# Second tables on ScalarE, another order at the end of a convolution's head, and one slot more between two transposes

## The chip, the cores and the metric

The kernel runs on one core of a Trainium2 chip. The metric is the device time of one execution in microseconds; lower is better. Five engines work side by side, each on its own list of instructions: TensorE (PE; its weight loads are shown as PEld), VectorE (DVE), ScalarE (ACT), GpSimd (POOL), and SyncE (SP), which here only issues DMA transfers. ACT issues some transfers too (ACTq).

## What is computed

```
u = x * v                                        # x, v: (2, 12480, 128) float32
h = (relu(pos_emb @ w1) @ w2) * exp(-0.01*pos)   # one filter for both batches
y = irfft(rfft(u, 2S) * rfft(h, 2S))[:, :S]      # S = 12480, along the sequence
z = (x * y).reshape(24960, 128)
g = z @ w_in                                     # w_in: (128, 2048)
out = max(0.01*g, g) @ w_out                     # w_out: (2048, 128)
```

## The kernel before

The long convolution is a Fourier transform in two steps (a matrix over one part of the index, a turn by phases, a matrix over the other part), and the rest is a two-layer network over 24960 tokens. In time:

- **Stage A** (0 to about 180 us) runs over 16 chunks `c`. It loads x, v and positions of batch 0, multiplies (`uh`), transforms (`a`, L370), adds and subtracts on VectorE (`o`, L106 and L108) and stores to DRAM. At c = 2 it loads the tables `mb` and `mi` of the second step. From c = 6 to 10 the generator `turned` (L160) is stepped once a chunk: it loads phases (`ph`, L164), forms products and sums of cosines and sines (`pr`, `cs`, L170 to L175), scales blocks of the identity by them (`rm`, L181), and from these builds a second set of tables with TensorE.
- **Stage B** (about 185 to 350 us) runs over 25 chunks of frequencies: the hidden layer of the filter (`ep` L714, `es` L717, `hp` L756), the forward matrix (`up` L123), the product with the filter (`ta`, `pin`, L131 and L132), then for the chunk before it the backward matrix (`dp`, L151, in `back_halves`). `dp` has two PSUM tiles, s = 0 and 1. Each is the sum of two matmuls, ri = 0 and 1, and each matmul has 64 rows: s = 0 uses rows 0 to 63 of `pin` and of the table, s = 1 rows 64 to 127. `back_evac` (L203) copies both to `ct`, and `store_back` (L199) stores `ct` in DRAM on ACT's queue. The preparation of the network's weights and pieces of batch 1's convolution (the generator `conv`; its matmuls are L408, its copies L104, its stores `scr1b` L421) are mixed in.
- **The end of the head** (347 to 366 us): the last chunk's `dp` and `ct`, the rows of `ct` that the first tile needs, straight into `cin` (`last_c`, L593), and the loads of the next tiles from what was stored (L565, L569, L586). Then tile 0: `join_hi` (L607) and `join_lo` (L616, L618) form `cp`, on VectorE for tile 0 and on GpSimd for all others; `front(0)` transforms (`yp`, L828), multiplies by x (`zt`, L831), transposes (`zp`, L836), and copies (`zf` L839 and L841, `zh` L847, `zl` L848), and the first matmul of the network, `mh` (L855), can start.
- **The main loop** runs over 50 blocks of 512 tokens times 16 slots, 800 slots. A slot `m1` has three matmuls (`mh`, L855 to L857), then relu and splitting on ACT and DVE; a slot `m2` three more (`acc`, L887 to L889), a few slots behind. The convolution's tiles t = 1 to 63 are fitted in between: `front(t)` in two halves, `yp` and `zt` three slots ahead of slot `ends[t]`, `zp` to `zl` at `ends[t]`; the joins 11 slots ahead (8 for the first two tiles of a batch); the loads at slots that follow from `ends` too. The list `ends` is made backwards: a tile is finished four slots before the block that needs it, and at least eight slots before the next tile. Each block's result is finished during the next block, in slots 2 to 6: `ot` at slot 2, transposes `op` (L911) and the copy `os` (L913) at slot 4, stores behind that. `yp`, `zp` and `op` share one PSUM buffer (tag `io`, one buffer), so each waits until the one before it has been read.

The lists are static: an engine takes its instructions in the order in which the program wrote them.

Of the kernel before, what the change touches and what calls it, by code (L numbers as in the profile page):

```python
# [8 lines left out]
F32 = mybir.dt.float32  # L9
# [4 lines left out]
ALU = mybir.AluOpType  # L14
# [16 lines left out]
def tile_conv_mlp(ctx, tc, x, v, pos_emb, w1, w2, w_in, w_out, cf, cr, cg, cb, ci, cw, out):  # L31
# [78 lines left out]
    def run(g):  # L110
        for _ in g:
            pass
# [32 lines left out]
    def back_halves(dp, pin, c):  # L145

        for j, w in halves(c):
            for ri in range(2):
                for s in range(2):
                    rows = slice(HB * s, HB * s + HB)  # L150
                    nc.tensor.matmul(dp[s][:, w], mi2[j][rows, ri, :], pin[rows, ri, w],  # L151
                                     start=(ri == 0), stop=(ri == 1))

# [5 lines left out]

    def turned(pool, psum, m2, m1):  # L160

        ph = pool.tile([128, 2, 2], F32, tag="ph0", name="ph0", bufs=1)
        for h in range(2):
            nc.sync.dma_start(out=ph[HB * h:HB * h + HB],  # L164
                              in_=cf[0, :, 0, :].rearrange("m (r k) -> m r k", r=2)[:, :, 0:KH + 1:KH])
        yield
        pr = pool.tile([128, 2, 2], F32, tag="pr", name="pr", bufs=1)
        cs = pool.tile([128, 3], F32, tag="cs", name="cs", bufs=1)
        tt = nc.vector.tensor_tensor
        tt(out=pr[:, 0, :], in0=ph[:, :, 1], in1=ph[:, :, 0], op=ALU.mult)  # L170
        tt(out=pr[:, 1, 0:1], in0=ph[:, 1, 1:2], in1=ph[:, 0, 0:1], op=ALU.mult)
        tt(out=pr[:, 1, 1:2], in0=ph[:, 0, 1:2], in1=ph[:, 1, 0:1], op=ALU.mult)
        tt(out=cs[:, 0:1], in0=pr[:, 0, 0:1], in1=pr[:, 0, 1:2], op=ALU.add)
        tt(out=cs[:, 1:2], in0=pr[:, 1, 1:2], in1=pr[:, 1, 0:1], op=ALU.subtract)
        tt(out=cs[:, 2:3], in0=pr[:, 1, 0:1], in1=pr[:, 1, 1:2], op=ALU.subtract)  # L175
        yield
        rm = pool.tile([128, 2, HB], F32, tag="rm", name="rm", bufs=1)
        for h, a, b in ((0, 0, 1), (1, 2, 0)):
            r = slice(HB * h, HB * h + HB)
            for i, q in enumerate((a, b)):  # L180
                nc.vector.tensor_scalar_mul(rm[r, i, :], ident[r, r], cs[r, q:q + 1])  # L181
        yield
        tp = psum()
        for i, t in enumerate((m2[:, 0], m2[:, 1], m1[:, 0], m1[:, 1])):
            nc.tensor.transpose(tp[:, i, :], t, ident)
        ts = pool.tile([128, 4, 128], F32, tag="ts", name="ts", bufs=1)
        nc.scalar.copy(ts, tp)
        yield
        rp = psum()
        for i in range(4):  # L190
            nc.tensor.matmul(rp[:, i, :], ts[:, i, :], rm.rearrange("p r m -> p (r m)"), start=True, stop=True)
        nc.scalar.copy(mi2[1], rp[:, 0:2])
        nc.scalar.copy(mi_h[1], rp[:, 2:4])
        nc.vector.tensor_tensor(out=mi_l[1], in0=rp[:, 2:4], in1=mi_h[1], op=ALU.subtract)
        yield
# [3 lines left out]
        eng.dma_start(out=scr2[b][k0:k0 + n].rearrange("k r m e -> (r m) k e"),  # L199
                          in_=ct[:, :n].rearrange("p k s d -> p k (s d)"))  # L200

    def back_evac(dp, ct, n, other=None):

        for s in range(2):
            (s and other or nc.scalar.copy)(ct[:, :n, s, :], dp[s][:, :n * D].rearrange("p (k d) -> p k d", d=D))
            yield


    with tc.manual_schedule():
# [22 lines left out]
        with ExitStack() as st:  # L232
# [81 lines left out]
            for c in range(NC0):  # L314
                if c + 3 < NC0:
                    load_a(c + 3)
                    if (c + 3) * MC % PQ == 0:
                        load_pos((c + 3) * MC // PQ)
                if c == 2:
                    nc.sync.dma_start(out=mb, in_=cb)  # L320
                    nc.sync.dma_start(out=mi, in_=ci)
                    for s in range(2):
                        for ri in range(2):
                            nc.sync.dma_start(out=mi2[0][HB * s:HB * s + HB, ri], in_=ci[HB * ri:HB * ri + HB, s])
                if c == 6:
                    nc.scalar.mul(mi, mi, 1 / 0.99)
                    for m, mh, ml in ((mb.rearrange("p s r q -> p s (r q)"), mb_h, mb_l), (mi, mi_h[0], mi_l[0])):
                        nc.scalar.copy(mh, m)
                        nc.vector.tensor_tensor(out=ml, in0=m, in1=mh, op=ALU.subtract)
                    turn_ = turned(sba, lambda: psa.tile([128, 4, 128], F32, tag="pp", name="tp"), mi2[0], mi)  # L330
                if 6 <= c < 11:
                    next(turn_, None)
                for f in late:
                    f()
# [286 lines left out]
        with ExitStack() as st:  # L621
# [97 lines left out]
            def evac(c):  # L719
                ct = sbb.tile([128, KC, 2, D], F32, tag="ct", name="ct", bufs=2)  # L720
                k0, n = chunk(c)
                end = c == ORD[-1]
                run(back_evac(dps.pop(c), ct, n, nc.vector.tensor_copy if end else None))
                if c in ORD[-2:]:
                    last_c(ct, k0, n, (nc.sync, nc.scalar if end else nc.sync))
                store_back(0, c, ct, nc.scalar)

            eh, dps = {}, {}
            first_c = upper_c(0)
# [54 lines left out]
                    f()  # L784
                late.clear()

            ahead(A1)
            dps[ORD[-1]] = two("d")
            back_halves(dps[ORD[-1]], pins.pop(ORD[-1]), ORD[-1])
            evac(ORD[-1])  # L790
            load_c(1)
            mult_a(2)
            ahead(A2)
            run(wprep)
            ahead(A3)


# [126 lines left out]
        first = [next(pieces_of(t))[0] for t in range(total)]  # L924
        ends, e = {}, NTL * NF
        for t in reversed(range(1, total)):
            e = min(e - 8, first[t] * NF - 4)
            ends[t] = e
        steps = {}

# [33 lines left out]
        SLOTS = ends[NT] - 14  # L964
        done = AHEAD
        frt = front(0)
        join_hi(0)
        join_lo(0)
        next(frt)
        load_tile(2)  # L970
        fetch_a(3)
        for _ in range(4 * A4):
            next(conv)
        run(frt)
        for _ in range(4 * A5):
# [98 lines left out]
```

## Time and profile before

| | us |
|---|---|
| median of three runs | 1732.74 |
| fastest, slowest | 1730.29, 1736.19 |
| profiled execution, its own time | 1735.8 |
| span of its instructions | 1734.0 |
| stage A, stage B, end of head, main loop (about) | 180, 170, 19, 1368 |

Times in the profile count from the start of the span. A row of a timeline has the start, the busy time, the engine, the line in the kernel, the operation with what it writes and reads, and in square brackets how long the engine had been idle and what released it. A row of a list of waits has who waited for whom: the total in us, how often, and the longest. A matmul of 4-byte data (L151, L408, L828) shows as two records, each with its weight load, so its counts in the trace are twice the program's.

### The profile page before, as it was taken

How to read it: one execution, taken by the hardware profiler on the slowest of the kernel's cores; microseconds unless marked ns; L12 is line 12 of the kernel's file. 1: busy time of each engine (PE TensorE's matmuls, PEld its weight loads, DVE VectorE, ACT ScalarE, POOL GpSimd, SP SyncE). 2: the span in 40 equal slices, each digit the busy share in tenths (PEclk: the TensorE clock that was granted, in tenths of full speed). 3: DMA queues.
4: the chain of work that ended last, by engine and by line, in shares of the span. 5: the costliest groups of instructions: out<-in, count | busy, mean ns of one | idle time of the engine just before them, and what ended most of it. 6: DMA issues, size and time to landing. Idle time of an engine off the chain costs nothing.

```text
span 1734.0 us, 27418 instructions
## 1 busy us (share of the span) xinstructions
PE 1650.2 (95%) x9185; PEld 1327.1 (77%) x9185; DVE 1108.7 (64%) x1705; ACT 985.4 (57%) x2005; POOL 833.0 (48%) x858
## 2 busy tenths in 40 slices
PE   6788799889999999999999999999999999999998
PEld 5777455478888887877788777877787878787878
DVE  3586588744554565555555554577777777777775
ACT  1222354434444466666667666566666666666666
POOL 3444122243444277777768675343644454345430
PEclk9889899989999999999999999999999999999999
DMA  8898899964665475556565551222212122111200
GB/s 225 247 263 242 281 322 331 306 201 148 206 182 175 120 200 160 167 154 194 149 175 167 157 150 64 77 67 62 65 43 81 44 70 70 60 53 56 73 18 20
DMA packets 166679, 253.27 MB, mean 146 GB/s; under 512 B 14622, under 2 KB 119346, under 8 KB 163466
## 3 DMA queue, kind: packets, MB, share of 16 engines
q1 hardware_dynamic: 146378, 225.81, 44.8%
q10 hardware_dynamic: 20160, 25.70, 4.3%
q8 instruction: 73, 1.20, 0.3%
q14 instruction: 68, 0.56, 0.1%
HBM read 167.95 MB, written 83.43 MB: 145 GB/s over the span
## 4 chain that ended last, share of the span: by engine, by line
PE 78%; DMA 9%; DVE 5%; issue 3%; SPq 2%; ACT 2%; POOL 1%; ACTq 0%; POOLq 0%; DVEq 0%
PE mh L855 11%; PE mh L857 10%; PE mh L856 10%; PE acc L889 10%; PE acc L887 10%; PE acc L888 10%; PE cv L137 4%; PE yp L828 4%; PE cv L408 3%; DMA ft<-in_cf_dram 2%; DMA xt<-in_x_dram 2%; PE op L911 2%; DMA scr<-o 1%; PE zp L836 1%; DMA scr<-ct 1%
## 5 line engine op out<-in xcount | busy, mean ns | idle before, releaser
L862 DVE SCALAR_TENSOR_TENSOR rl<-mh,rh 128x512 fp32r<-128x512 f32 (+2 forms) x400 | 270.1, 677 | 311.3 <-ACT rh L861 306.9
L872 DVE TENSOR_TENSOR rl<-r,rh 128x512 fp32r<-128x512 f32 (+1 forms) x400 | 329.5, 837 | 113.3 <-ACT rh L871 105.7
L861 ACT ACTIVATE rh<-mh 128x512 fp32r<-128x512 f32 (+2 forms) x400 | 235.2, 590 | 211.7 <-PE mh L857 197.3
L867 ACT ACTIVATE r<-mh 128x512 f32<-128x512 f32 (+1 forms) x400 | 235.7, 590 | 184.8 <-PE mh L857 168.0
L855 PE MATMUL mh<-zh,w_in_h 128*128 128x512 f32 (+3 forms) x800 | 329.8, 412 | 1.9 <-ACT zh L847 1.3
L857 PE MATMUL mh<-zh,w_in_l 128*128 128x512 f32 (+3 forms) x800 | 310.5, 388 | 0.0
L887 PE MATMUL acc<-rh,w_out_h 128*128 128x512 f32 (+3 forms) x800 | 310.3, 388 | 0.0
L856 PE MATMUL mh<-zl,w_in_h 128*128 128x512 f32 (+3 forms) x800 | 310.0, 388 | 0.0
L889 PE MATMUL acc<-rh,w_out_l 128*128 128x512 f32 (+3 forms) x800 | 310.0, 388 | 0.0
L888 PE MATMUL acc<-rl,w_out_h 128*128 128x512 f32 (+3 forms) x800 | 308.3, 385 | 0.0
L848 POOL TENSOR_TENSOR zl<-zf,zh 128x390 fp32r<-128x390 f32 (+24 forms) x110 | 75.7, 702 | 349.7 <-ACT zh L847 349.5
L618 POOL TENSOR_TENSOR cp<-cq,cp 98x256 f32<-98x256 f32 x252 | 212.4, 843 | 19.8
L607 POOL TENSOR_TENSOR cp<-cin 98x256 f32<-98x256 f32 x126 | 104.5, 850 | 162.8 <-PE yp L828 118.7
L855 PEld LDWEIGHTS mh<-zh,w_in_h 128*128 128x128 f32 x800 | 151.1, 189 | 37.0 <-issue 9.9
L857 PEld LDWEIGHTS mh<-zh,w_in_l 128*128 128x128 f32 x800 | 150.8, 189 | 32.1
L888 PEld LDWEIGHTS acc<-rl,w_out_h 128*128 128x128 f32 x800 | 150.4, 188 | 32.1 <-DVE rl L872 0.6
L889 PEld LDWEIGHTS acc<-rh,w_out_l 128*128 128x128 f32 x800 | 150.3, 188 | 31.5
L887 PEld LDWEIGHTS acc<-rh,w_out_h 128*128 128x128 f32 x800 | 150.4, 188 | 30.4
L856 PEld LDWEIGHTS mh<-zl,w_in_h 128*128 128x128 f32 x800 | 151.5, 189 | 24.5 <-POOL zl L848 0.7
L869 DVE CAST rh<-r 128x512 fp32r<-128x512 f32 (+1 forms) x200 | 114.3, 572 | 38.4 <-ACT r L867 35.8
L871 ACT CAST rh<-r 128x512 fp32r<-128x512 f32 (+1 forms) x200 | 122.1, 611 | 6.4
L616 POOL TENSOR_TENSOR cq<-cin 98x256 f32<-98x256 f32 x126 | 113.3, 899 | 1.0 <-DMA cin<-scr 1.0
(154 smaller groups left out, 2359.0 us busy)
## 6 DMA issues: line engine op xcount, KB each, us to landing
cin<-scr SPq DMA_DIRECT2D x318, 98.0 KB
hd<-hspec SPq DMA_DIRECT2D x48, 512.0 KB
scr<-o SPq DMA_DIRECT2D x32, 588.0 KB
bin<-scr SPq DMA_DIRECT2D x23, 768.0 KB
scr1b<-o SPq DMA_DIRECT2D x32, 392.0 KB
hspec<-hs ACTq DMA_DIRECT2D x48, 256.0 KB
scr<-ct ACTq DMA_DIRECT2D x24, 512.0 KB
xm<-in_x_dram SPq DMA_DIRECT2D x128, 96.0 KB
```

The source lines that it names most:

```text
L618: eng.tensor_tensor(out=cp[:, p, w], in0=cq[:, p], in1=cp[:, p, 1], op=op)
L855: nc.tensor.matmul(hp, w_in_h[:, fs], zh, start=True, stop=False)
L856: nc.tensor.matmul(hp, w_in_h[:, fs], zl, start=False, stop=False)
L857: nc.tensor.matmul(hp, w_in_l[:, fs], zh, start=False, stop=True)
L861: nc.scalar.activation(out=rh, in_=hp, func=AF.Relu)
L862: nc.vector.scalar_tensor_tensor(out=rl, in0=hp, scalar=0.0, in1=rh, op0=ALU.max, op1=ALU.subtract)
L867: nc.scalar.activation(out=r, in_=hp, func=AF.Lrelu, alpha=0.01)
L871: nc.scalar.copy(rh, r)
L872: nc.vector.tensor_tensor(out=rl, in0=r, in1=rh, op=ALU.subtract)
L887: nc.tensor.matmul(ap, w_out_h[:, f, :], rh, start=(f == 0 and at0[k] >= S), stop=False)
L888: nc.tensor.matmul(ap, w_out_h[:, f, :], rl, start=False, stop=False)
L889: nc.tensor.matmul(ap, w_out_l[:, f, :], rh, start=False, stop=(f == NF - 1))
```

## The change

Four edits.

1. `back_halves` runs s in the outer loop and ri in the inner one: both matmuls of rows 0 to 63 come first, then both of rows 64 to 127. This holds for all 25 chunks of stage B.
2. `turned`: the products, sums and scaled blocks are made by ScalarE (12 small operations) instead of VectorE; `ph` is loaded as 50 contiguous numbers of each of two parts rather than two numbers picked out of each; its load is issued at c = 2, ahead of `mb` and `mi`, and all later steps come one chunk earlier (c = 6 to 9).
3. End of the head: both copies of the last `ct` are ScalarE's (the second was VectorE's); its store goes on SP's queue, behind the rows of `last_c`, instead of ACT's; seven pieces of `conv` come before the last `dp` and one behind `evac` (eight before), which moves the `scr1b` stores behind those rows; `join_hi(0)` stands ahead of the next pieces, and one more piece stands ahead of `join_lo(0)`.
4. Tiles are seven slots apart instead of eight. In 16 places, where two tiles fall to one block (t = 1, 5, 9, 13, 17, 21, 26, 30, 32, 36, 40, 44, 48, 53, 57, 61), the earlier of the two moves one slot back.

The core of the diff:

```
     def back_halves(dp, pin, c):
         for j, w in halves(c):
-            for ri in range(2):
-                for s in range(2):
-                    rows = slice(HB * s, HB * s + HB)
+            for s in range(2):
+                rows = slice(HB * s, HB * s + HB)
+                for ri in range(2):
                     nc.tensor.matmul(dp[s][:, w], mi2[j][rows, ri, :], pin[rows, ri, w],
                                      start=(ri == 0), stop=(ri == 1))
...
     def turned(pool, psum, m2, m1):
-        ph = pool.tile([128, 2, 2], F32, tag="ph0", name="ph0", bufs=1)
+        ph = pool.tile([128, 2, KH + 1], F32, tag="ph0", name="ph0", bufs=1)
         for h in range(2):
             nc.sync.dma_start(out=ph[HB * h:HB * h + HB],
-                              in_=cf[0, :, 0, :].rearrange("m (r k) -> m r k", r=2)[:, :, 0:KH + 1:KH])
+                              in_=cf[0, :, 0, :].rearrange("m (r k) -> m r k", r=2)[:, :, :KH + 1])
         yield
...
-        tt(out=pr[:, 0, :], in0=ph[:, :, 1], in1=ph[:, :, 0], op=ALU.mult)
-        tt(out=pr[:, 1, 0:1], in0=ph[:, 1, 1:2], in1=ph[:, 0, 0:1], op=ALU.mult)
...
+        for i, (a, b, c, d) in enumerate(((c1, c0, s1_, s0_), (c0, s1_, c1, s0_))):
+            nc.scalar.mul(pr[:, i:i + 1], a, b)
+            if i:
+                nc.scalar.mul(pr[:, 2:3], c, d)
+                nc.scalar.mul(pr[:, 2:3], pr[:, 2:3], -1.0)
+                nc.scalar.add(cs[:, 2:3], pr[:, 1:2], pr[:, 2:3])
+                nc.scalar.mul(cs[:, 1:2], cs[:, 2:3], -1.0)
+            else:
+                nc.scalar.mul(pr[:, 2:3], c, d)
+                nc.scalar.add(cs[:, 0:1], pr[:, 0:1], pr[:, 2:3])
...
-                nc.vector.tensor_scalar_mul(rm[r, i, :], ident[r, r], cs[r, q:q + 1])
+                nc.scalar.mul(rm[r, i, :], ident[r, r], cs[r, q:q + 1])
...
                 if c == 2:
+                    turn_ = turned(sba, lambda: psa.tile([128, 4, 128], F32, tag="pp", name="tp"), mi2[0], mi)
+                    next(turn_)
                     nc.sync.dma_start(out=mb, in_=cb)
...
-                if 6 <= c < 11:
+                if 6 <= c < 11 - 1:
                     next(turn_, None)
...
-                run(back_evac(dps.pop(c), ct, n, nc.vector.tensor_copy if end else None))
+                run(back_evac(dps.pop(c), ct, n))
                 if c in ORD[-2:]:
                     last_c(ct, k0, n, (nc.sync, nc.scalar if end else nc.sync))
-                store_back(0, c, ct, nc.scalar)
+                store_back(0, c, ct, nc.sync if end else nc.scalar)
...
-            ahead(A1)
+            for _ in range(4 * A1 - 1):
+                next(conv)
             dps[ORD[-1]] = two("d")
             back_halves(dps[ORD[-1]], pins.pop(ORD[-1]), ORD[-1])
             evac(ORD[-1])
+            next(conv)
...
             run(wprep)
+            join_hi(0)
             ahead(A3)
...
-            e = min(e - 8, first[t] * NF - 4)
+            e = min(e - 7, first[t] * NF - 4)
...
-        join_hi(0)
+        next(conv)
         join_lo(0)
         next(frt)
         load_tile(2)
         fetch_a(3)
-        for _ in range(4 * A4):
+        for _ in range(4 * A4 - 1):
             next(conv)
```

Where instructions move, three places show it. Lines of the changed kernel stand four to eight higher: L593 becomes L598, L199 L203, L421 L426, L565 L570, L408 L413, L828 L836, L836 L844, L855 L863, L887 L895, L911 L919.

SP's queue at the end of the head, before (`cin<-ct` are the last rows, `scr1b` batch 1's piece, `cin<-scr` the loads of the next tile):

```order
L593 DMA cin<-ct 4x1x256 x4
L421 DMA scr1b<-o_1371 98x4x256 x2
L593 DMA cin<-ct 4x1x256 x2
L565 DMA cin<-scr_0_63 49x512 x3
L569 DMA cin<-scr_0_63 49x2x128 x2
L586 DMA cin<-scr_0_63 49x512 x2
```

and after:

```order
L598 DMA cin<-ct 4x1x256 x6
L203 DMA scr_0_63<-ct 128x4x256
L426 DMA scr1b<-o_1373 98x4x256 x2
L570 DMA cin<-scr_0_63 49x512 x3
L574 DMA cin<-scr_0_63 49x2x128 x2
L591 DMA cin<-scr_0_63 49x512 x2
```

The piece's two stores went behind the rows, and the store of `ct` came onto this queue between them.

TensorE from the last `dp` to the first matmuls of the network, before (`hp` and `cv` are pieces of batch 1):

```order
L151 MATMUL dp<-pin,mi_75 128x512 x4
L408 MATMUL hp<-xv_2940,ft_2938 98x128 x8
L828 MATMUL yp<-cp,gt 64x128 x8
L408 MATMUL cv<-xv_2940,ft_2938 98x128 x8
L836 MATMUL zp<-ident,zt 128x113 x4
L855 MATMUL mh<-zh,w_in_h 128x390
L856 MATMUL mh<-zl,w_in_h 128x390
L857 MATMUL mh<-zh,w_in_l 128x390
L855 MATMUL mh<-zh,w_in_h 128x390
L856 MATMUL mh<-zl,w_in_h 128x390
L857 MATMUL mh<-zh,w_in_l 128x390
L828 MATMUL yp<-cp,gt 64x128 x8
```

and after:

```order
L151 MATMUL dp<-pin,mi_75 128x512 x4
L413 MATMUL hp<-xv_2942,ft_2940 98x128 x8
L413 MATMUL cv<-xv_2942,ft_2940 98x128 x8
L836 MATMUL yp<-cp,gt 64x128 x8
L844 MATMUL zp<-ident,zt 128x113 x4
L863 MATMUL mh<-zh,w_in_h 128x390
L864 MATMUL mh<-zl,w_in_h 128x390
L865 MATMUL mh<-zh,w_in_l 128x390
L863 MATMUL mh<-zh,w_in_h 128x390
L864 MATMUL mh<-zl,w_in_h 128x390
L865 MATMUL mh<-zh,w_in_l 128x390
```

`cv` moved from between `yp` and `zp` to ahead of `yp`; the `yp` of tile 1 now stands behind a third group of `mh`.

TensorE at a block where two tiles meet, before:

```order
L836 MATMUL zp<-ident,zt 128x113 x4
L911 MATMUL op<-ident,ot 98x128 x4
L855 MATMUL mh<-zh,w_in_h 128x512
L856 MATMUL mh<-zl,w_in_h 128x512
L857 MATMUL mh<-zh,w_in_l 128x512
L887 MATMUL acc<-rh,w_out_h 128x512
L888 MATMUL acc<-rl,w_out_h 128x512
L889 MATMUL acc<-rh,w_out_l 128x512
```

and after:

```order
L919 MATMUL op<-ident,ot 98x128 x4
L863 MATMUL mh<-zh,w_in_h 128x512
L864 MATMUL mh<-zl,w_in_h 128x512
L865 MATMUL mh<-zh,w_in_l 128x512
L895 MATMUL acc<-rh,w_out_h 128x512
L896 MATMUL acc<-rl,w_out_h 128x512
L897 MATMUL acc<-rh,w_out_l 128x512
L844 MATMUL zp<-ident,zt 128x113 x4
```

`zp` moved from directly ahead of `op` to a slot of six matmuls behind it.

## Rows read from the trace of the kernel before

**Rows 1.** The page, busy time: engine, us, share of the span, instructions.

```profile
PE 1650.2 (95%) x9185; PEld 1327.1 (77%) x9185; DVE 1108.7 (64%) x1705; ACT 985.4 (57%) x2005; POOL 833.0 (48%) x858
```

**Rows 2.** Waits of PE, 372 to 1060 us: total us, times, longest.

```profile
PE op L911 <- ACT zf L841: 5.2, 7, 0.8
```

**Rows 3.** Waits of PE, 1110 us to the end.

```profile
PE op L911 <- ACT zf L841: 5.5, 7, 0.8
PE yp L828 <- POOL cp L618: 1.2, 2, 0.8
```

**Rows 4.** Timeline around 1104 us, GpSimd: start, us, engine, line, operation [idle before <-releaser].

```profile
1104.46 1.03 POOL L848 TENSOR_TENSOR zl<-zf,zh 128x390 fp32r<-128x390 f32 x1 [18.32 <-ACT zh L847]
1105.44 1.45 POOL L607 TENSOR_TENSOR cp<-cin 98x256 f32<-98x256 f32 x2
```

**Rows 5.** Timeline around 1250 us, a block where two tiles meet.

```profile
1249.67 0.55 PE L836 MATMUL zp<-ident,zt 113*128 113x113 f32 x4
1250.61 0.35 ACT L841 COPY zf<-zp 128x196 f32<-128x196 f32 x1
1251.01 0.64 PE L911 MATMUL op<-ident,ot 128*98 128x128 f32 x4 [0.79 <-ACT zf L841]
...
1251.41 0.48 PE L855 MATMUL mh<-zh,w_in_h 128*128 128x512 f32 x1
...
1251.69 0.59 ACT L913 COPY os<-op 98x512 f32<-98x512 f32 x1 [0.18 <-PE op L911]
...
1252.65 0.39 PE L889 MATMUL acc<-rh,w_out_l 128*128 128x512 f32 x1
```

**Rows 6.** Timeline of the end of the head.

```profile
350.98 0.90 SPq L421 DMA_DIRECT2D scr1b<-o  x2
...
351.99 2.34 SPq L593 DMA_DIRECT2D cin<-ct  x2
352.92 1.40 ACTq L199 DMA_DIRECT2D scr<-ct  x1
...
357.83 2.78 PE L828 MATMUL yp<-cp,gt 98*64 98x128 f32 x16 [6.28 <-issue]
...
360.54 3.73 PE L408 MATMUL cv<-xv,ft 98*98 98x128 f32 x16
...
364.07 0.96 PE L836 MATMUL zp<-ident,zt 113*128 113x113 f32 x4
...
365.60 1.82 POOL L618 TENSOR_TENSOR cp<-cq,cp 98x256 f32<-98x256 f32 x2
...
366.29 0.69 PE L855 MATMUL mh<-zh,w_in_h 128*128 128x390 f32 x1 [1.26 <-ACT zh L847]
```

**Rows 7.** A stretch of the end: length; busy PE, PEld, DVE, ACT, POOL; clock; DMA.

```profile
356.00:360.00 4.00, 2.17 (x15) 1.79 (x16) 3.31 (x9) 0.00 (x0) 0.00 (x0) 0.50 0.53 170
```

**Rows 8.** Groups of PE by line in stage B, 190 to 350 us: busy us, mean ns.

```profile
L151 PE MATMUL dp<-pin,mi 64*128 64x512 f32 (+3 forms) x208 | 48.8, 590 | 0.0
```

**Rows 9.** Timeline of the last `dp`, its second and third pair of records.

```profile
348.18 0.59 PE L151 MATMUL dp<-pin,mi 64*128 64x512 f32 x2
```

```profile
348.61 0.59 PE L151 MATMUL dp<-pin,mi 64*128 64x512 f32 x2
```

**Rows 10.** Waits of PE in stage B, 190 to 350 us.

```profile
PE hp L756 <- ACT es L717: 5.8, 4, 3.2
PE up L123 <- DVE ta L131: 5.2, 9, 2.7
```

**Rows 11.** Timeline of stage A, steps of `turned`.

```profile
85.71 2.27 SPq L164 DMA_DIRECT2D ph<-in_cf_dram  x2
...
90.90 1.50 DVE L170 TENSOR_TENSOR pr<-ph 128x2 f32<-128x2 f32 x1
92.33 0.15 DVE L171 TENSOR_TENSOR pr<-ph 128x1 f32<-128x1 f32 x1
92.40 1.68 DVE L172 TENSOR_TENSOR pr<-ph 128x1 f32<-128x1 f32 x1
```

More of the change, by code (lines that the diff above doesn't have):

```diff
@@ L160, in turned @@
     def turned(pool, psum, m2, m1):
-        ph = pool.tile([128, 2, 2], F32, tag="ph0", name="ph0", bufs=1)
+        ph = pool.tile([128, 2, KH + 1], F32, tag="ph0", name="ph0", bufs=1)
         for h in range(2):
             nc.sync.dma_start(out=ph[HB * h:HB * h + HB],
-                              in_=cf[0, :, 0, :].rearrange("m (r k) -> m r k", r=2)[:, :, 0:KH + 1:KH])
+                              in_=cf[0, :, 0, :].rearrange("m (r k) -> m r k", r=2)[:, :, :KH + 1])
         yield
-        pr = pool.tile([128, 2, 2], F32, tag="pr", name="pr", bufs=1)
+        (c0, c1), (s0_, s1_) = ([ph[:, r, k:k + 1] for k in (0, KH)] for r in range(2))
+        pr = pool.tile([128, 3], F32, tag="pr", name="pr", bufs=1)
         cs = pool.tile([128, 3], F32, tag="cs", name="cs", bufs=1)
-        tt = nc.vector.tensor_tensor
-        tt(out=pr[:, 0, :], in0=ph[:, :, 1], in1=ph[:, :, 0], op=ALU.mult)
-        tt(out=pr[:, 1, 0:1], in0=ph[:, 1, 1:2], in1=ph[:, 0, 0:1], op=ALU.mult)
[L172 to L175, printed above, removed]
+        for i, (a, b, c, d) in enumerate(((c1, c0, s1_, s0_), (c0, s1_, c1, s0_))):
[8 more added lines that the diff above has]
+                nc.scalar.add(cs[:, 0:1], pr[:, 0:1], pr[:, 2:3])
         yield
@@ L200, in store_back, with back_evac @@
                           in_=ct[:, :n].rearrange("p k s d -> p k (s d)"))
-    def back_evac(dp, ct, n, other=None):
+    def back_evac(dp, ct, n):
         for s in range(2):
-            (s and other or nc.scalar.copy)(ct[:, :n, s, :], dp[s][:, :n * D].rearrange("p (k d) -> p k d", d=D))
+            nc.scalar.copy(ct[:, :n, s, :], dp[s][:, :n * D].rearrange("p (k d) -> p k d", d=D))
             yield
@@ L329, in tile_conv_mlp @@
                         nc.vector.tensor_tensor(out=ml, in0=m, in1=mh, op=ALU.subtract)
-                    turn_ = turned(sba, lambda: psa.tile([128, 4, 128], F32, tag="pp", name="tp"), mi2[0], mi)
-                if 6 <= c < 11:
+                if 6 <= c < 11 - 1:
                     next(turn_, None)
```

## The prediction

> **What bounds the kernel now.** I read the page's busy times first: TensorE is busy 95% of the span, 1650 us, and no other engine is over 64% [rows 1]. So an edit is worth what it takes out of TensorE's idle time, or adds to its work. I then asked who TensorE waits for, by stage. In the main loop nearly all of its waiting has one shape: the transposes `op` wait for ScalarE's copy `zf`, 5.2 us in 7 times before 1060 us and 5.5 us in 7 times after 1110 us [rows 2, 3]. In stage B TensorE is the bound too, with some waits for `es` and for `ta` (5.8 and 5.2 us) that other late things can hide in [rows 10]. The end of the head is a chain of single steps across all engines, and there TensorE stands idle, 6.28 us ahead of `yp` alone [rows 6]. Stage A waits for transfers; a change there counts only if it touches what the transfers wait for.
>
> **Pairs seven slots apart.** In the timeline of such a block `zp` runs at 1249.67, ScalarE's last `zf` at 1250.61 for 0.35 us, and `op`, which needs the same PSUM buffer, can start at 1251.01 only, after 0.79 us of idle TensorE [rows 5]. The change puts a slot of six matmuls between `op` and `zp`, so `op` finds the buffer long read. 14 such waits make 5.2 + 5.5 = 10.7 us, 0.76 each [rows 2, 3]; the 15th falls between the two stretches and I count it at the same 0.76: 11.5 us. The 16th moved tile is t = 1, at the very start, with no `op` beside it. Now `zp` must wait until `os` has read `op`. In the row `os` starts 0.68 us after `op` and takes 0.59, so the buffer is free 1.27 us after `op` starts, while 0.40 us from `op` to the first matmul and a slot of six matmuls, about 1.4 us (the first starts at 1251.41, the sixth at 1252.65), pass before `zp` [rows 5]. The margin is about half a microsecond; I expect no wait, and allow 1 us over all pairs for ScalarE being late now and then. GpSimd gains too: at tile 33 its join stood behind `zl` of tile 32, which waited 18.32 us for `zh` [rows 4], and a `yp` then waited up to 0.8 us [rows 3]; the join now comes first, 0.8 us. Sum: -11.5 - 0.8 + 1.0 = **-11.3 us**, between -12.5 (no new wait, a little of the second `yp` wait too) and -8 (a new wait of 0.3 us at each pair).
>
> **End of the head.** Two things stood in the way of tile 0. First, SP issued batch 1's two stores at 350.98, for 0.90 us, ahead of the last two rows of `cin`, which started at 351.99 and took 2.34 us to issue behind them [rows 6]. Now the rows go first: 1.0 us earlier at least, 2.3 at most if the slow issue was the stores' doing. Second, `cv` ran on TensorE for 3.73 us from 360.54, between `yp` and `zp`. `yp` ended at 360.61 (357.83 + 2.78); without `cv` the multiplication by x lies between, about 0.9 us, so `zp` could start at 361.5 rather than 364.07: 2.6 us [rows 6]. `cv` itself now fits into the 6.28 us in which TensorE had nothing to do ahead of `yp` [rows 6]. Together 3.6 to 4.9 us at `mh`, which started at 366.29. What is late next is tile 1: its join on GpSimd ended at 367.42 (365.60 + 1.82) [rows 6], and its loads wait for the store of `ct`, which was issued at 352.92 on ScalarE's queue and now follows six rows on SP's, about a microsecond earlier at best. With `mh` from about 362 and three groups of `mh` ahead of the `yp` of tile 1 instead of two, TensorE comes to it near 366, and the join ends near 366.4: up to a microsecond of the gain is lost there. The granted clock was 0.50 in this stretch (356 to 360) [rows 7], the lower of TensorE's two levels, and it stays there for some 10 us of work in either order, so I take no gain from the clock. I take **-3.8 us**, between -5.6 (the join is early too) and -1.5 (the rows land when they did, and tile 1 waits).
>
> **Second tables on ScalarE.** VectorE loses 3.2 us in two operations of one or two numbers per row, 1.50 and 1.68 us, where the one between them takes 0.15 [rows 11]. SP loses 2.27 us for `ph` at c = 6 [rows 11], and issues a like transfer at c = 2. ScalarE gets twelve small operations; its duration for such is not in these rows, and ScalarE, busy 57% of the span [rows 1], has room in this stage. Stage A waits for transfers, so I count half of VectorE's 3.2 us: **-1.5 us**, between -3 (all of it, in the chain of `o`) and +1.5 (two thirds of the 2.27 us of issue, now ahead of c = 2's loads).
>
> **Order of the halves.** The four matmuls of a `dp` show as eight records that start two at a time, 0.43 us apart (348.18, 348.61) [rows 9]. In program order neighbours alternate between rows 0 to 63 and rows 64 to 127, so the trace shows that neighbours on different rows run side by side. The new order puts two matmuls of the same rows next to each other, which no row shows. Three prices are possible for each of 24.5 full chunks (208 records are 26 groups of eight [rows 8]; one of the 25 chunks is split in two groups, and the last has half the width): nothing, if the third matmul starts beside the first; 0.86 us, if matmuls start in program order, since then the first runs alone, the second and third together and the fourth alone, 6 starts of 0.43 us instead of 4; 1.72 us if nothing overlaps. I take **nothing**, because the two records of one matmul already let the neighbour's first record start between them (two start together, two more 0.43 us later, with four matmuls of two records): the two halves of the array evidently work off their own lists. That is an inference from start times, not a measurement, and it is the largest uncertainty here.
>
> The Trainium skill, "TensorE: Matmul & The Clock Gate", Part 3 "Packing small matmuls", "The mechanism", speaks against this edit: weight loads overlap running matmuls only where the row groups differ, and matmuls start and end in program order. By that rule the middle price holds; no run here shows it yet for this order.
>
> **Sum.** -11.3 - 3.8 - 1.5 + 0 = -16.6 us on the profiled execution's 1735.8 us: 1719.2. That execution was 3.1 us over the median of the three runs, 1732.74; taken off, **1716.1 us**.
>
> **Rivals.**
> *Program order in the halves.* 24.5 x 0.86 = 21.1 us more work for TensorE in stage B. The waits there, 5.8 and 5.2 us [rows 10], lie in the same chunks and could take up to 11.0 of it, so +10.1 to +21.1; the middle, 15.6, gives 1716.1 + 15.6 = **1731.7**. For it: that no row shows same-row neighbours overlapping with anything. Against: the interleaved starts above. By the rule of the Trainium skill named above this rival is the outcome.
> *No overlap at all*, the one that ends slower: 24.5 x 1.72 = 42.1, less the 11.0 of waits, +31: **1747**. It decides from the point where a same-row successor also holds back the next row half's weight load, so that none of the four runs beside another. Against it: the second and third of the new order still use different rows.
> *A new wait at the pairs.* If `zp` one slot later waits for `os` as long as `op` waited for `zf`, the 11.5 us come back: **1727.6**. For it: one shared buffer, and ScalarE takes `os` between relu work. Against: the half microsecond of margin above.
>
> **How the numbers follow.** Chances: forecast 0.55, program order 0.32, no overlap 0.08, new wait 0.05. A measurement of this kernel can tell 0.3%, some 5.2 us, from no change: faster is under 1727.5, slower over 1737.9. The forecast's own range, from the bounds above, is 1711 to 1725, all faster. Of program order a fifth (1726 to 1728) is faster and the rest within; the new wait is half and half. Faster: 0.55 + 0.06 + 0.02 = 0.63; within: 0.26 + 0.03 = 0.29; slower 0.08. The range goes from the low end of the forecast, 1711 less half a microsecond, to 1735, well into program order; left out are no overlap (0.08), the top of program order (0.06), and a tail below (0.05).
>
> **What would show it.** Pairs: no wait of `op` for `zf` in the main loop, and none of `zp` for `os`. Head: `yp` starts near 356, `cv` stands ahead of it, the first `mh` starts 3.6 to 4.9 us earlier against the last `dp`. Tables: no operation of `turned` on VectorE, and the chunks at c = 6 to 8 some 1.5 us shorter. Halves: eight records of L151 that still start at four times, 0.43 us apart, or at six times with single ones at both ends. I am wrong if the stretch from 190 to 347 us grows by 10 us or more, or if a new wait of 0.3 us or more shows at each of the pairs.

## The result, and the profile after

The changed kernel took 1710.99 us (median of four runs, 1708.96 to 1713.04), the kernel before 1733.6 beside it (four runs). The ratio is 0.9867, 95% interval 0.9847 to 0.9887, so about 23 us faster. The same program timed once more came to 0.9876 (0.9857 to 0.9894). The prediction was 1716.1 us, faster, with 1710.5 to 1735; the measured time lies inside, half a microsecond above the lower end, and the saving is larger than the 16.6 us forecast. The direction and the main cause were right; sizes of single terms were not, and one step of the head did not come out. One execution of one of the variants below (2040.4 us, at a mean granted clock of 0.749 where all others had 0.975 to 0.984) is left out of its median.

The profiled execution of the changed kernel took 1712.6 us, its span is 1710.8. Where [rows 1] had TensorE at 95%:

```profile
span 1710.8 us, 27419 instructions
PE 1645.7 (96%) x9185; PEld 1326.7 (78%) x9185; DVE 1107.7 (65%) x1694; ACT 987.3 (58%) x2018; POOL 832.6 (49%) x858
```

The waits of TensorE from 365 us to the end (who waits, for whom: total us, times, longest) answer to [rows 2, 3]:

```profile
PE mh L863 <- DVE rl L870: 0.7, 1, 0.7
PE op L919 <- ACT ot L910: 0.5, 1, 0.5
PE yp L836 <- POOL cp L623: 0.4, 1, 0.4
PE yp L836 <- POOL usp L501: 0.3, 1, 0.3
```

and in the kernel before, the same view from 372 us on:

```profile
PE op L911 <- ACT zf L841: 11.4, 15, 0.8
PE yp L828 <- POOL cp L618: 1.2, 2, 0.8
PE mh L855 <- DVE rl L862: 0.6, 1, 0.6
PE op L911 <- ACT ot L902: 0.5, 1, 0.5
```

All 15 waits of `op` for `zf` are gone, no `zp` waits for `os`, and 1.9 us of waiting are left in about 1350. The timeline of TensorE at a block where two tiles meet, beside [rows 5]:

```profile
1232.03 0.60 PE L919 MATMUL op<-ident,ot 128*98 128x128 f32 x4
1232.38 0.48 PE L863 MATMUL mh<-zh,w_in_h 128*128 128x512 f32 x1
...
1233.86 0.55 PE L844 MATMUL zp<-ident,zt 113*128 113x113 f32 x4
1234.18 0.48 PE L863 MATMUL mh<-zh,w_in_h 128*128 128x512 f32 x1
```

The reader is to look at starts, not at busy times. `op` takes 0.35 us until the next matmul starts (1232.03 to 1232.38), `zp` 0.32 (1233.86 to 1234.18), 0.67 together. In [rows 5] both together, from the start of `zp` at 1249.67 to the matmul at 1251.41, took 1.74.

The end of the head, beside [rows 6]:

```profile
344.22 1.99 PE L151 MATMUL dp<-pin,mi 64*128 64x512 f32 x8
...
346.24 1.07 ACT L209 COPY ct<-dp 128x512 f32<-128x512 f32 x2 [0.88 <-PE dp L151]
...
347.34 2.06 ACTq L598 DMA_DIRECT2D cin<-ct  x2
348.57 0.46 SPq L203 DMA_DIRECT2D scr<-ct  x1
349.13 1.54 SPq L426 DMA_DIRECT2D scr1b<-o  x2
349.50 0.58 ACT L104 COPY a1s<-hp 98x512 f32<-98x512 f32 x1 [2.19 <-issue]
...
351.56 2.59 PE L413 MATMUL cv<-xv,ft 98*98 98x128 f32 x16 [3.42 <-DVE o L108]
352.00 0.42 DVE L621 TENSOR_TENSOR cq<-cin 98x256 f32<-98x256 f32 x1 [0.59 <-issue]
...
353.71 0.88 DVE L623 TENSOR_TENSOR cp<-cq,cp 98x256 f32<-98x256 f32 x2
...
354.07 1.98 PE L836 MATMUL yp<-cp,gt 98*64 98x128 f32 x16
...
356.84 1.01 PE L844 MATMUL zp<-ident,zt 113*128 113x113 f32 x4 [0.79 <-DVE zt L839]
...
359.12 0.69 PE L863 MATMUL mh<-zh,w_in_h 128*128 128x390 f32 x1 [1.26 <-ACT zh L855]
```

`cv` stands in the hole ahead of `yp`, `zp` follows `yp` at 2.77 us from start to start instead of 6.24, and from the last `dp` to the first `mh` pass 14.9 us. The last `dp` still shows eight records in 1.99 us. (`a1s` is ScalarE's copy ahead of the sums `o`, both of batch 1's piece; `cq` is the first step of tile 0's `join_lo`.)

### The profile page after: what moved, and what is told of

Same layout as the page of the kernel before. It is cut to its first block, busy times and chain, and to the rows that moved or that the text cites. A ratio compares the mean times of both kernels' runs of the same rounds, so it can differ in the third digit from the quotient of the medians.

```text
span 1710.8 us, 27419 instructions
## 1 busy us (share of the span) xinstructions
PE 1645.7 (96%) x9185; PEld 1326.7 (78%) x9185; DVE 1107.7 (65%) x1694; ACT 987.3 (58%) x2018; POOL 832.6 (49%) x858
## 4 chain that ended last, share of the span: by engine, by line
PE 82%; DMA 10%; DVE 5%; SPq 1%; issue 1%; POOL 1%; ACT 0%; ACTq 0%; DVEq 0%; POOLq 0%
PE mh L863 11%; PE acc L895 10%; PE acc L897 10%; PE mh L865 10%; PE mh L864 10%; PE acc L896 10%; PE cv L137 4%; DMA xt<-in_x_dram 4%; PE yp L836 4%; PE cv L413 3%; PE op L919 2%; PE zp L844 1%; PE up L123 1%; DVE ta L131 1%; DMA scr<-o 1%
## 5 line engine op out<-in xcount | busy, mean ns | idle before, releaser
L880 DVE TENSOR_TENSOR rl<-r,rh 128x512 fp32r<-128x512 f32 (+1 forms) x400 | 337.1, 858 | 107.3 <-ACT rh L879 99.9
L875 ACT ACTIVATE r<-mh 128x512 f32<-128x512 f32 (+1 forms) x400 | 235.2, 588 | 177.0 <-PE mh L865 160.1
L863 PE MATMUL mh<-zh,w_in_h 128*128 128x512 f32 (+3 forms) x800 | 329.7, 412 | 2.0 <-ACT zh L855 1.3
L895 PE MATMUL acc<-rh,w_out_h 128*128 128x512 f32 (+3 forms) x800 | 310.4, 388 | 0.0
L863 PEld LDWEIGHTS mh<-zh,w_in_h 128*128 128x128 f32 x800 | 151.0, 189 | 35.0 <-issue 7.5
L895 PEld LDWEIGHTS acc<-rh,w_out_h 128*128 128x128 f32 x800 | 150.4, 188 | 30.3
```

Source lines behind the costliest of these rows:

```text
L863: nc.tensor.matmul(hp, w_in_h[:, fs], zh, start=True, stop=False)
L875: nc.scalar.activation(out=r, in_=hp, func=AF.Lrelu, alpha=0.01)
L880: nc.vector.tensor_tensor(out=rl, in0=r, in1=rh, op=ALU.subtract)
L895: nc.tensor.matmul(ap, w_out_h[:, f, :], rh, start=(f == 0 and at0[k] >= S), stop=False)
```

## The experiments

All times below are medians beside the kernel before on the same chip; "saves" is the ratio to it turned into us, with its 95% interval. The ratio is not that of the two medians, and the two can differ by some 3 us.

**The spacing alone.**

```
-            e = min(e - 8, first[t] * NF - 4)
+            e = min(e - 7, first[t] * NF - 4)
```

> The kernel before with the seven-slot spacing alone. The two traces so far show the main loop 16.0 us shorter from the first to the last matmul of the network, where the idle time of TensorE that the profile names came to 12.1 us less. Theory A (a stall costs more than the idle time shown, because the busy time of the matmuls ahead of it includes a tail that overlaps the next one otherwise): -15 to -16.5 us, and 0.95 to 1.0 us at each of the late pairs. Theory B (only the named idle time belongs to the spacing, the other 4 us come from tile 1 and the head): -11 to -12.5 us.

Measured: 1716.64 against 1733.32 us, ratio 0.9914 (0.9895 to 0.9933): it saves 14.9 us (11.6 to 18.2). The spacing carries about two thirds of the whole. The interval does not tell the two theories apart, but the traces do: see the table of stages below, where the main loop is some 16.4 us shorter in every kernel with seven slots.

**The order of the halves alone.**

```
-            for ri in range(2):
-                for s in range(2):
-                    rows = slice(HB * s, HB * s + HB)
+            for s in range(2):
+                rows = slice(HB * s, HB * s + HB)
+                for ri in range(2):
```

> The kernel before with the new order in back_halves alone. Theory A (the two row halves of the array work off their own lists): within 1 us of before, records of L151 still start in pairs, 0.43 us apart. Theory B (program order): +10 us or more, six starts in a group. Theory C (the new order costs something small at each chunk and explains the 4.4 us that stage B lost between the traces): +3 to +5 us.

Measured: 1731.72 against 1733.32, ratio 0.9999 (0.9987 to 1.0010), nothing within 2.3 us. In stage B the line's group, 188 to 350 us (busy us, mean ns), answers to [rows 8]:

```profile
L151 PE MATMUL dp<-pin,mi 64*128 64x512 f32 (+3 forms) x208 | 49.1, 590 | 0.0
```

The records of a `dp` still start in pairs 0.43 us apart, as in [rows 9]. The second and third pair of the last `dp`, in the changed kernel, which has the same order:

```profile
344.75 0.60 PE L151 MATMUL dp<-pin,mi 64*128 64x512 f32 x2
```

```profile
345.18 0.60 PE L151 MATMUL dp<-pin,mi 64*128 64x512 f32 x2
```

Theory A stands; program order (B) would have cost 10 us or more, and C 3 to 5.

**The end of the head alone** (all of edit 3 in the change above, nothing else).

```
-                run(back_evac(dps.pop(c), ct, n, nc.vector.tensor_copy if end else None))
+                run(back_evac(dps.pop(c), ct, n))
...
-                store_back(0, c, ct, nc.scalar)
+                store_back(0, c, ct, nc.sync if end else nc.scalar)
...
+            join_hi(0)
             ahead(A3)
...
-        join_hi(0)
+        next(conv)
         join_lo(0)
```

> The kernel before with the edits at the end of the head alone. Theory A (the chain from the last dp to the first mh is what they shorten, by itself): -3 to -4.5 us, first mh of the network about 4 us earlier against the last dp, yp near 356. Theory B (tile 1 then waits on GpSimd's join and takes it back): -1 to 0 us.

Measured: 1733.48 against 1733.32, ratio 1.0006 (0.9994 to 1.0017): nothing, at most 1 us gained. In its trace the first `mh` comes 15.0 us after the last `dp`, as in the changed kernel, so the first half of theory A is right, though its `yp` starts 10.0 us after the last `dp`, where the kernel before had 10.2: the sign "`yp` near 356", some two microseconds earlier, did not come. And the gain is gone 21 slots later. The timeline of TensorE there:

```profile
360.10 0.53 PE L860 MATMUL mh<-zh,w_in_l 128*128 128x390 f32 x1
360.56 1.44 PE L831 MATMUL yp<-cp,gt 98*64 98x128 f32 x8
362.37 1.92 PE L831 MATMUL yp<-cp,gt 98*64 98x128 f32 x8 [0.37 <-POOL cp L618]
364.22 0.69 PE L858 MATMUL mh<-zh,w_in_h 128*128 128x390 f32 x1
```

The `yp` of tile 1 takes 3.66 us from its start to the next matmul, where that of tile 0 ran its 16 records in 1.98 at the same clock in the changed kernel: it goes as fast as GpSimd's join delivers `cp`. That is theory B, for 1.7 us. The rest goes with the clock, below.

**The tables alone** (all of edit 2).

```
-        tt(out=pr[:, 0, :], in0=ph[:, :, 1], in1=ph[:, :, 0], op=ALU.mult)
...
+            nc.scalar.mul(pr[:, i:i + 1], a, b)
...
-                if 6 <= c < 11:
+                if 6 <= c < 11 - 1:
```

> The kernel before with the second tables' edit alone. Theory A (stage A really is some 7 us shorter by this edit and stage B gives back about 4 at its transfers): first up of stage B 6 to 8 us earlier, whole time -2.5 to -4 us. Theory B (the 7.5 us in stage A were chance of that one execution): first up within 2 us of before in this profile, whole time -1.5 to 0 us. Theory C (nothing given back with the old order of halves): -6 to -8 us.

Measured: 1730.97 against 1733.32, ratio 0.9992 (0.9980 to 1.0004): it saves 1.4 us, between 3.5 saved and 0.7 lost. The whole time is theory B's; C is out. The first `up` came at 174.7, 6.5 us before that of the kernel before, which is theory A's sign; but the start of stage B, which lay 7.5 us apart between the traces of before and of the changed kernel, turned out to move by that much in kernels whose stage A is word for word that of before (the table of stages below). So that sign tells nothing. The eight small products and sums show on ScalarE in 0.2 to 0.3 us each, and the four scaled blocks in 0.34. Two of the rows, from the changed kernel's timeline:

```profile
78.75 0.29 ACT L171 ACTIVATE pr<-ph 128x1 f32<-128x1 f32 x1
...
90.18 1.18 ACT L185 ACTIVATE rm<-ident,cs 64x64 f32<-64x64 f32 x4
```

**Spacing and head together** (edits 3 and 4).

> The kernel before with the spacing and the end of the head together. Alone they gave about -15 and 0 us. Theory A (they help each other: with seven slots the yp of tile 1 stands behind one more group of mh, so the head's 3.6 us at the first mh are kept): -18 to -20 us, and from the first mh to the sixth nothing lost against the changed kernel. Theory B (they only add; the changed kernel's other 7 us come from elsewhere): -14 to -16 us. In either, the time at which TensorE's granted clock is back at 1.00 is to be read: in the changed kernel that was 3.8 us after the first mh, with the head alone 10.5 us after it.

Measured: 1716.28 against 1732.67, ratio 0.9913 (0.9899 to 0.9927): 15.1 us, no more than the spacing alone. Theory B. Its one trace looked better than that, with the clock back 4 to 5 us after the first `mh`; five runs say that a single trace is no measure of 3 us here.

**The stores of the spectrum behind `es`**, on the changed kernel.

```
-                for s in range(2):
-                    nc.scalar.dma_start(out=hspec[c][:, :, s, :n * D], in_=hs[HB * s:HB * s + HB, :, :n * D])
                 if i + 1 < NCH:
                     hidden(ORD[i + 1])
+                for s in range(2):
+                    nc.scalar.dma_start(out=hspec[c][:, :, s, :n * D], in_=hs[HB * s:HB * s + HB, :, :n * D])
```

> The changed kernel with the two stores of the filter's spectrum issued on ScalarE behind the copy es of the next chunk instead of ahead of it. Theory A (late in stage B, ScalarE's list stands at an issue that waits for transfers, es and then TensorE wait for it, 6.6 us in the trace of the changed kernel, and this gives back what is gained earlier): 3 to 6 us faster than the changed kernel, the waits of hp for es under 1.5 us. Theory B (the transfers themselves are the bound there, busy share 1.0): within 1 us, the wait moves to another name.

Measured: 1710.94 against 1732.67, ratio 0.9870 (0.9857 to 0.9884); the changed kernel had 0.9867 and 0.9876. No difference in time. The waits of TensorE in stage B did change. The changed kernel, 183 to 346 us:

```profile
PE hp L761 <- ACT es L722: 6.6, 2, 3.7
PE up L123 <- DVE ta L131: 4.4, 8, 2.0
```

with the stores behind `es`, 180 to 345 us:

```profile
PE up L123 <- DVE ta L131: 9.0, 13, 3.4
PE ep L719 <- DMA bin<-scr: 0.8, 1, 0.8
PE hp L761 <- ACT es L722: 0.7, 1, 0.7
```

The wait for `es` went, as theory A says, and much of it came back as a wait for `ta`; in time it is theory B. In this one trace the last `dp` came some 5 us earlier than in the others, but the four times do not show it, so I don't claim it.

**How far TensorE looks past matmuls of the same rows.** Each matmul of `dp` cut into four of 128 columns, once with all eight of rows 0 to 63 first, once alternating. Same work, more and smaller instructions.

```
-            for s in range(2):
-                rows = slice(HB * s, HB * s + HB)
-                for ri in range(2):
-                    nc.tensor.matmul(dp[s][:, w], mi2[j][rows, ri, :], pin[rows, ri, w],
+            cuts = [slice(q, min(q + D, w.stop)) for q in range(w.start, w.stop, D)]
+            for s in range(2):
+                rows = slice(HB * s, HB * s + HB)
+                for v in cuts:
+                    for ri in range(2):
+                        nc.tensor.matmul(dp[s][:, v], mi2[j][rows, ri, :], pin[rows, ri, v],
```

> The changed kernel with each full-width matmul of dp cut into four of 128 columns, and all eight of rows 0 to 63 ahead of all eight of rows 64 to 127. Theory A (each half's list goes on however far the other half's first matmul stands behind): a chunk's group as long as with alternating quarters. Theory B (TensorE looks ahead over a limited number of instructions): the second half starts late, a group takes up to 3.5 us instead of about 2.0, and the whole time grows by up to 30 us.

> The same quarters with the row halves alternating: the control for the run before it. A group of 32 records in pairs, 2.0 to 2.4 us; whole time within 10 us of the changed kernel.

Measured, one execution each: 1738.89 us by halves, 1717.01 alternating. The group of L153 on TensorE from 185 to 375 us by halves, and then alternating (busy us, mean ns):

```profile
L153 PE MATMUL dp<-pin,mi 64*128 64x128 f32 x784 | 88.2, 285 | 0.0
```

```profile
L153 PE MATMUL dp<-pin,mi 64*128 64x128 f32 x784 | 50.5, 278 | 0.0
```

And the timeline of one chunk by halves, then of one chunk alternating:

```profile
254.26 3.16 PE L153 MATMUL dp<-pin,mi 64*128 64x128 f32 x29
257.15 0.37 PE L763 MATMUL hp<-w,es 64*128 64x128 f32 x1
257.26 0.27 PE L153 MATMUL dp<-pin,mi 64*128 64x128 f32 x1
257.37 0.27 PE L763 MATMUL hp<-w,es 64*128 64x128 f32 x1
```

```profile
250.18 2.06 PE L153 MATMUL dp<-pin,mi 64*128 64x128 f32 x32
```

Theory B, for eight in a row: the 32 records take 3.5 us (254.26 to the last at 257.48 plus its 0.27) instead of 2.06. They run singly at steps of 0.11 us, and only a few pair up at the change of halves: 3.16 us for 29 records, less the last one's 0.27, are 26 steps. Where the next matmul, `hp`, is on the other rows, it runs beside the last three records of `dp`. Record by record, the second half's first starts at 255.71, beside the thirteenth of the first half (255.70), when three of that half's sixteen are still to come; in 24 of the 25 groups of this trace it starts with exactly three to come. So TensorE passed three records of the same rows here, and not four. Two matmuls of 4-byte data are four records; three of them stand between the first record of one half and the first of the other, and that is just within this reach. Each quarter variant ran once, but the length of a group is the same in 22 of 25 (3.5 us) and in 24 of 25 (2.06 us).

**Leaving one part out of the changed kernel**, all four beside each other. The edits are those above, undone one at a time.

> The changed kernel once more, beside the three that follow. So far it measured -23 us from four runs, where the spacing and the head measured -15 and the other two edits alone -1.4 and 0. Theory A (the parts add up, and the first four runs lay low): -16 to -18 us. Theory B (the parts help each other): -21 to -24 us again.

> The changed kernel with the old making of the second tables. Theory A (parts add): 1 to 2 us slower than the changed kernel. Theory B (the tables' edit is worth more once the rest is there, since stage B no longer hides it): 4 to 6 us slower.

> The changed kernel with the old order in back_halves. Theory A (parts add, the order is free): within 1 us of the changed kernel. Theory B (with both copies on ScalarE the order by halves lets the first copy start earlier): 2 to 4 us slower.

> The changed kernel with the old end of the head. Theory A (the head's gain at the first mh is eaten by what follows, as it was alone): within 1 us of the changed kernel. Theory B (with seven slots it is kept): 3 to 4 us slower.

Measured, against 1734.33 us: all parts 1713.48, ratio 0.9876 (0.9857 to 0.9894); without the tables 1716.43, 0.9912 (0.9892 to 0.9933); without the halves 1712.74, 0.9880 (0.9862 to 0.9898); without the head 1717.06, 0.9896 (0.9880 to 0.9912). All parts save 21.5 us again, theory B's number. The halves are free here too, theory A. Without the tables the kernel is 3.0 us slower by the medians and 6.2 by the ratios, without the head 3.6 and 3.5, theory B for both by most of these figures; the intervals overlap that of all parts, by little for the tables.

**The stages in all traces.** One execution each, us: the start of the first `up` of stage B; of the last `dp`; of the first `mh`; the time from the last `dp` to the first `mh`; from there to the 21st `mh` slot; and from that to the last `acc` slot.

```
                    first up  last dp  first mh |  head  21 slots  main loop
before                 181.2    347.6     366.3 |  18.6    29.7     1331.7
halves alone           176.8    344.4     362.1 |  17.8    30.0     1333.2
head alone             174.8    342.8     357.9 |  15.0    32.8     1331.9
tables alone           174.7    345.1     362.9 |  17.9    30.5     1331.8
spacing alone          176.1    343.9     361.6 |  17.7    30.0     1315.4
spacing + head         173.8    343.3     359.3 |  16.0    29.0     1315.4
without head           176.5    346.8     363.9 |  17.1    29.2     1315.6
without tables         173.8    344.4     359.4 |  15.0    30.1     1315.2
without halves         175.6    343.8     359.4 |  15.6    29.9     1315.6
changed                173.7    344.2     359.1 |  14.9    30.3     1315.1
changed again          177.0    343.4     358.8 |  15.3    31.8     1315.4
es first               176.6    338.6     354.7 |  16.0    29.3     1315.3
```

Read by columns. The main loop has two values, 1331.7 to 1333.2 with eight slots, 1315.1 to 1315.6 with seven. The head has two, 17.1 to 18.6 with the old end (mean 17.8), 14.9 to 16.0 with the new (mean 15.4). The first `up` has none: with the old tables it comes at 173.8 to 176.8 and once, in the profiled execution of before, at 181.2; with the new at 173.7 to 177.0. And whatever it is, the last `dp` comes at 342.8 to 347.6, the stores behind `es` left aside: an early start of stage B is not an early end. The transfers may be what paces it (the busy share of the DMA engines was 0.98 to 0.99 from 300 to 330 us in the changed kernel); no run shows that.

## Why the prediction came out, point by point

**Pairs seven slots apart: right mechanism, wrong size.** Predicted -11.3 us, between -12.5 and -8; the traces show -16.4, outside that range. Three terms were off.
- The price of a stall. I took the 0.76 us of idle time that the profile names. But the profile counts a matmul as busy to its modelled end, and of the 0.55 us of `zp` in [rows 5] only 0.32 are spent when another matmul follows at once. From start to start, `zp` and `op` together went from 1.74 us to 0.67, 1.07 less; a second restart of `mh` costs 0.1, since the first of a group behind transposes takes 0.32 until its successor starts instead of 0.23. Slot by slot the two traces differ by 0.8 to 1.1 us at the pairs, mostly 0.94 to 1.0. 15 x 0.97 = 14.5 us.
- The second `yp` wait, at tile 33. I counted 0.8; both parts of it went, 1.2 us of idle time, and from start to start the step is shorter by 1.86 us. That GpSimd's join must come ahead of `zl` of tile 32 was right: it starts right after the `yp` of tile 32 and ends before that `zl`, where in [rows 4] it came after one.

```profile
1086.65 1.44 POOL L612 TENSOR_TENSOR cp<-cin 98x256 f32<-98x256 f32 x2 [4.24 <-PE yp L836]
...
1091.18 1.56 POOL L623 TENSOR_TENSOR cp<-cq,cp 98x256 f32<-98x256 f32 x2
1092.69 1.03 POOL L856 TENSOR_TENSOR zl<-zf,zh 128x390 fp32r<-128x390 f32 x1
```

- The new wait of `zp` for `os`. I allowed 1 us; there is none. The margin of half a microsecond was enough. That rival is refuted.

14.5 + 1.9 = 16.4 us; the stage table has 16.4 between the medians of its two groups. The whole time of the spacing alone says 14.9 (11.6 to 18.2), which agrees.

**End of the head: the second step right, the first not.** Predicted -3.8 us, range -5.6 to -1.5. The stage table gives 17.8 - 15.4 = 2.4 us at the first `mh`. The two profiled executions alone give 3.7, nearly the forecast, but that is luck: the kernel before was at its slowest there (18.6 against a mean of 17.8). The traces of the table, cut at the end of tile 0's `yp`, tell the two steps apart.

- *`cv` off the path*: from the end of `yp` to the first `mh` pass 5.68 us in four of the five traces with the old end (5.45 in the fifth), and 3.06 to 3.07 in all seven with the new one. That is the predicted 2.6.
- *The rows first*: from the last `dp` to the end of `yp` pass 12.2 us in the mean with the old end (11.7 to 13.0), and 12.4 with the new (11.8 to 13.0). I expected 1.0 to 2.3 less, and this is the step that failed, in two ways. First, SP's six rows are out 1.1 to 2.4 us earlier now, but two more rows go out on ScalarE's queue, no earlier than before (5.2 us after the last `dp`). And SP's rows were not the only late thing in the kernel before. There VectorE went without a break from batch 1's sums into tile 0's, and batch 1's waited for `a1s`, which ScalarE began 0.04 us after it had issued its rows and the store of `ct` (352.92 + 1.40 in [rows 6]); SP ended its issue in the same moment (351.99 + 2.34), so the trace does not say which of the two would have been the later:

```profile
354.36 0.59 ACT L104 COPY a1s<-hp 98x512 f32<-98x512 f32 x1 [4.11 <-DMA cin<-ct]
...
355.59 0.68 DVE L108 TENSOR_TENSOR o<-hp,a1s 98x512 f32<-98x512 f32 x1
...
356.19 0.75 DVE L607 TENSOR_TENSOR cp<-cin 98x256 f32<-98x256 f32 x2
356.85 0.42 DVE L616 TENSOR_TENSOR cq<-cin 98x256 f32<-98x256 f32 x1
```

With the new end VectorE stands idle for 0.59 us ahead of `cq`, probably for ScalarE's two rows, and tile 0's sums are done 0.6 us earlier in the mean (10.4 instead of 11.0 us after the last `dp`). Second, `cv` did not fit into the hole for nothing. It waits for `o` (3.42 us), and that again for `a1s` behind ScalarE's issue of rows, so it starts 7.3 to 7.4 us after the last `dp` in all seven traces and takes 2.6 to 3.7. `yp` must follow it and ends 1.4 to 2.6 us after the last of the sums, where it ended 1.2 after them with the old end. That takes the 0.6 back.

What I named as next late, tile 1 on GpSimd, is what the head alone ran into. How much remains in the total is not settled: alone the edit cost 1.0 us (1.0 saved to 2.9 lost), with the spacing it saved nothing more than the spacing alone, and taken out of the changed kernel it cost 3.5 with overlapping intervals.

**The clock.** I took no gain from it, and in total none shows, but it moves more than the edit does. I put the stretch at the lower level at some 10 us in either order; it was 17 us in the kernel before (355.2 to 372.3), and between two executions of the same changed program it differs. Columns as in [rows 7]: length, busy times, the granted clock third from the right. In the first the clock, 0.50 and so the lower of TensorE's two levels since about 353 us, is back between 362 and 364:

```profile
362.00:364.00 2.00, 1.47 (x12) 0.78 (x10) 1.13 (x2) 0.74 (x2) 1.84 (x4) 0.76 0.61 184
364.00:366.00 2.00, 1.64 (x12) 1.22 (x13) 0.55 (x1) 0.00 (x0) 1.16 (x2) 1.00 0.52 122
```

in the second only after 368:

```profile
366.00:368.00 2.00, 2.00 (x7) 2.00 (x7) 0.56 (x1) 0.50 (x1) 1.92 (x3) 0.50 1.00 253
368.00:370.00 2.00, 2.00 (x11) 2.00 (x11) 0.47 (x1) 0.50 (x1) 1.84 (x4) 0.86 0.96 274
```

and its 21 slots took 31.8 us instead of 30.3. With the head alone the clock came back at about 368 too, 10 us after the first `mh`, and the 21 slots took 32.8. So it seems that work which is pulled forward into a stretch of low clock is partly paid back by running slower; no run holds the clock fixed to show it.

**Tables: right alone, more beside the other parts.** Predicted -1.5, range -3 to +1.5; alone 1.4 us (-3.5 to +0.7). The size was a guess, half of VectorE's 3.2 us, and no stage of the traces shows it: the last `dp` comes at 342.8 to 347.6 with the old tables, 343.4 to 346.8 with the new (the stores behind `es` left aside), and shorter chunks in stage A can't be told from the spread of its end. Nor do the 3.2 us look like the price of the two operations. Both ran beside a GpSimd operation and ended within 0.03 us of its end (92.40 and 94.08 in [rows 11]), while the one between took 0.15:

```profile
90.00 2.38 POOL L263 TENSOR_TENSOR uh<-xt,vt 98x1024 f32<-98x1024 f32 x1 [1.90 <-DMA ph<-in_cf_dram]
92.32 1.74 POOL L272 TENSOR_TENSOR q<-ft,rot 98x784 f32<-98x784 f32 x1
```

Beside the spacing and the head the edit seems worth more than its range allows. The two kernels that have both of these but not the tables save 15.1 and 15.3 us, the four that have all three 20.8 to 23.1. Over all executions, the 14 of the changed kernel and of the one without the halves have a mean of 1712.3 us, the ten without the tables 1717.0: 4.7 less (1.8 to 7.6), on chips whose kernel before lies within 1.7 us. The table of stages can't show where that comes from, since the profiled executions of the two kernels without the tables were the fastest of their kernels (1711.74 and 1712.76). I leave the cause open.

**Order of the halves: right.** Predicted 0; -0.2 us alone (-2.3 to +1.7); undone, the changed kernel is 0.7 us slower by the ratios and 0.7 faster by the medians. Eight records of L151 still take 1.99 us and start in four pairs, so both halves are at work all the time though the third matmul stands behind two of the other half. Program order, my rival at 0.32, would have taken about 2.85 (six starts 0.43 us apart and a tail of 0.27), and no overlap more. The Trainium skill, "TensorE: Matmul & The Clock Gate", Part 3 "Packing small matmuls", "The mechanism", says that matmuls start and end in program order. The trace does not agree where row halves differ: the third matmul starts beside the first, ahead of the second. But the quarters show that my reason, two lists that run independently, was too generous: with eight in a row the halves do run one after the other but for three records, 3.5 against 2.06 us a chunk. The new order is free because it stays just inside that reach, which I did not know.

**The sum.** The forecast was 16.6 us; measured were 23 (19.6 to 26.5) and 21.5 (18.4 to 24.8), so the range held and the size did not. Of the terms, the spacing gave 5 us more in the traces, the head 1.4 less at the first `mh`. The parts timed alone do not add up to the whole: 14.9 - 1.0 + 1.4 + 0.2 = 15.5, each uncertain by 2 to 3 us. The 6 to 7.5 us between appear when the tables join the spacing and the head, and none of my terms foresaw that.

## What to carry to other kernels

Price a stall of TensorE from start to start of the matmuls around it, against a place where the same steps follow without a wait; the idle time that the profile shows was 0.76 us a place where 0.97 came back. When a transfer is issued earlier, ask first whether the work behind it stood waiting for that transfer: here it hung on ScalarE's list as well, and the 1.0 to 2.3 us did not come. Before a difference between two traces is explained, look at the same stretch in a kernel whose code there is unchanged: some 6 of the 7.5 us in stage A were the draw of one execution (181.2 against a mean of 175.1 in the five others with the old tables). And a gain ahead of a stretch that is paced by transfers, or of one that runs at the lower clock, must be followed to the other side of it before it is counted.

## What the runs showed of the hardware

Two matmuls of 64 rows each, on different halves of the rows, run side by side even when the program has both matmuls of one half first; with eight of one half first they don't: the second half starts when three records of the first are still to come. Here three records were passed, never four. The granted clock of TensorE after a hole in its work stayed at 0.50 for 10 us in one execution (352.7 to 363.0) and 17 in another (351.5 to 368.6) of the same program. A copy on ScalarE that stands behind its issue of two transfers waits for that issue: 2.06 us in the changed kernel, and the copy began 0.1 us after it.
